# Row-tiled attention scores, stationary exponentials and 0/1 masks in a block-sparse attention with a feed-forward layer behind it

## The chip, the cores and the metric

The kernel runs on one core of one Trainium2 chip. The metric is the device time of one execution in microseconds. Before the change it is 330.93 us (median of 3 runs, 328.9 to 332.64). A lower time is better.

## The reference, cut to what matters

Four batches, eight heads, 768 positions, head size 64. Queries may see keys in blocks of 32: neighbours, the first and last block, and three sampled blocks per query block. The mask is the same for every head and batch. The attention output, with its heads side by side, goes through a feed-forward layer with squared relu.

```python
scores = scale * np.matmul(q, k.transpose(0, 1, 3, 2))
mask = np.abs(blk_i - blk_j) <= 1                       # block = 32
mask = mask | (blk_i == 0) | (blk_j == 0) | (blk_i == n_blocks - 1) | (blk_j == n_blocks - 1)
# ... sampled blocks are set to True per query block
scores = np.where(mask, scores, -1000000000.0)
attn = np.exp(scores - np.max(scores, axis=-1, keepdims=True))
attn = attn / (np.sum(attn, axis=-1, keepdims=True) + 1e-09)
out = np.matmul(attn, v)
# ... x = out with heads side by side: (4 * 768, 512)
h = x @ w_in                                             # 512 -> 2048
g = np.maximum(h, 0.0) ** 2
return g @ w_out                                         # 2048 -> 512
```

## The kernel before

Two heads make one unit, so there are 16 units, four per batch. A unit has three query chunks of 256 and, in each, three key pairs of 2 x 128 keys. One (unit, chunk, pair) is called a slot: 144 in all. Keys lie on the partitions of the scores, so that the exponentials are the moving operand of the second product as they come.

```python
# rows 0..63 of QK hold a head, rows 64..87 hold the mask as 24 more contraction rows
def scores(u, qi, cp):                                   # L319
    # ...
    for c in range(2):
        nc.tensor.matmul(ps[:, c, 0, :], KA[i][0:64 + nb, ksl], QA[i][0:64 + nb, qsl], start=True, stop=True)
        nc.tensor.matmul(ps[:, c, 1, :], KB[i][0:64 + nb, ksl], QB[i][0:64 + nb, qsl], start=True, stop=True)

def exps(u, qi, cp):                                     # ScalarE, 128 x 1024
    nc.scalar.activation(out=pT, in_=stile.pop((u, qi, cp)), func=AF.Exp, scale=scale)

def values(u, qi, cp):                                   # V stationary, half of its columns are ones
    # ...
        nc.tensor.matmul(po[:, 0, :], VA[i][:, n, :], pT[:, c, 0, :], ...)
        nc.tensor.matmul(po[:, 1, :], VB[i][:, n, :], pT[:, c, 1, :], ...)

def inverse(u, qi):                                      # 1/sum on ScalarE: Ln, Ln, Exp(-x)
    nc.scalar.activation(out=ls[0:D, :], in_=po[D:P, 0, :], func=AF.Ln)
    nc.scalar.activation(out=ls[D:P, :], in_=po[0:D, 1, :], func=AF.Ln)
    nc.scalar.activation(out=rs, in_=ls, func=AF.Exp, scale=-1.0)

def normalize(u, qi):                                    # two VectorE multiplies into xT
    V.tensor_mul(out=xT[b][0:D, a, qsl], in0=po[0:D, 0, :], in1=rs[0:D, :])
    V.tensor_mul(out=xT[b][D:P, a, qsl], in0=po[D:P, 1, :], in1=rs[D:P, :])
# feed-forward: hidden on TensorE, relu on VectorE, square on GpSimd, output on TensorE, copy on ScalarE
```

A small list scheduler in the kernel places all these tasks with estimated durations. It fixes the order on each engine when the program is built; every task has one engine.

The softmax here doesn't subtract the row's maximum and nothing guards it: scores larger than these inputs give would overflow.

## Time and profile before

| | before |
|---|---|
| span of the profiled execution | 332.6 us |
| TensorE matmul, busy share | 92% |
| VectorE, ScalarE, GpSimd busy | 157, 210, 129 us |
| matmuls | 2174 |
| DMA transposes | 48 |

The costliest groups of instructions in the page of the kernel before that the change removes or reshapes. A line gives source line, engine, operation, output<-input, shapes, count, then busy us and the mean ns of one, then the engine's idle time just before and what ended it.

```profile
L334 ACT ACTIVATE pT<-ps 128x1024 bf16<-128x1024 f32 x144 | 140.9, 1017 | 41.2 <-PE po L349 32.0
...
L347 PE MATMUL po<-pT,VA 128*128 128x256 bf16 x288 | 71.3, 274 | 7.7 <-DVE xT L368 4.6
L326 PE MATMUL ps<-QK 88*128 88x256 bf16 x288 | 72.6, 277 | 3.0 <-ACT pT L334 1.6
...
L367 DVE TENSOR_TENSOR xT<-po,rs 64x256 bf16<-64x256 f32 x48 | 19.9, 414 | 29.0 <-ACT rs L358 27.3
```

The mean of a matmul here is a latency: 274 ns for 256 columns that follow each other every 109 ns. The share of a matmul in the time is therefore not read from this column, but from the distance of starts. VectorE's wait on `rs` (27.3 us) is the three-step inversion on ScalarE in front of the normalization.

### The profile page before, as it was taken

How to read it: one execution, taken by the hardware profiler on the slowest of the kernel's cores; microseconds unless marked ns; L12 is line 12 of the kernel's file. 1: busy time of each engine (PE TensorE's matmuls, PEld its weight loads, DVE VectorE, ACT ScalarE, POOL GpSimd, SP SyncE). 2: the span in 40 equal slices, each digit the busy share in tenths (PEclk: the TensorE clock that was granted, in tenths of full speed). 3: DMA queues.
4: the chain of work that ended last, by engine and by line, in shares of the span. 5: the costliest groups of instructions: out<-in, count | busy, mean ns of one | idle time of the engine just before them, and what ended most of it. 6: DMA issues, size and time to landing. Idle time of an engine off the chain costs nothing. (4 is left out here: it accounts for less than half of the span.)

```text
span 332.6 us, 5743 instructions
## 1 busy us (share of the span) xinstructions
PE 306.5 (92%) x2174; PEld 209.8 (63%) x2174; DVE 156.6 (47%) x336; ACT 210.2 (63%) x317; POOL 129.3 (39%) x183
## 2 busy tenths in 40 slices
PE   2878899999978978999999999999999999999994
PEld 1555687777855756677776766777776655555541
DVE  7674244885454532366545334344334454444410
ACT  5479897859857778887786978888886301000011
POOL 6157143452422310055444232322223456666610
PEclk9999799999999999999999999999999999999999
DMA  7989995599999997482326200000000000100002
GB/s 228 233 195 206 199 289 211 120 250 229 216 285 239 246 271 225 95 204 42 62 67 73 55 2 32 2 32 3 32 33 1 34 33 32 63 34 32 34 32 96
DMA packets 59561, 39.61 MB, mean 119 GB/s; under 512 B 39790, under 2 KB 56462, under 8 KB 59534
## 3 DMA queue, kind: packets, MB, share of 16 engines
q1 hardware_dynamic: 55038, 34.66, 41.2%
q0 software_dynamic: 4224, 4.19, 7.8%
q10 hardware_dynamic: 272, 0.39, 0.3%
q8 instruction: 17, 0.28, 0.3%
q14 instruction: 10, 0.08, 0.1%
HBM read 27.26 MB, written 6.29 MB: 101 GB/s over the span
## 5 line engine op out<-in xcount | busy, mean ns | idle before, releaser
L395 POOL TENSOR_TENSOR g<-r 128x384 bf16<-128x384 f32 (+1 forms) x144 | 111.0, 776 | 175.7 <-DVE r L389 175.5
L334 ACT ACTIVATE pT<-ps 128x1024 bf16<-128x1024 f32 x144 | 140.9, 1017 | 41.2 <-PE po L349 32.0
L384 PE MATMUL ph<-xT,w_in_sb 128*128 128x384 bf16 (+1 forms) x576 | 120.0, 308 | 2.3 <-DVE r L389 2.1
L389 DVE TENSOR_SCALAR r<-ph 128x384 f32<-128x384 f32 (+1 forms) x144 | 73.1, 512 | 98.3 <-PE ph L384 72.8
L408 PE MATMUL py<-w_out_sb,g 128*128 128x512 bf16 x384 | 110.1, 379 | 0.8 <-ACT ys L413 0.8
L384 PEld LDWEIGHTS <-w_in_sb 128*128 128x128 bf16 x576 | 56.2, 98 | 38.2 <-issue 3.6
L347 PE MATMUL po<-pT,VA 128*128 128x256 bf16 x288 | 71.3, 274 | 7.7 <-DVE xT L368 4.6
L326 PE MATMUL ps<-QK 88*128 88x256 bf16 x288 | 72.6, 277 | 3.0 <-ACT pT L334 1.6
L328 PE MATMUL ps<-QK 88*128 88x256 bf16 x288 | 72.0, 276 | 0.4 <-DVE QK L285 0.2
L349 PE MATMUL po<-pT,VB 128*128 128x256 bf16 x288 | 71.1, 274 | 0.0
L413 ACT COPY ys<-py 128x512 f32<-128x512 f32 x24 | 13.9, 585 | 62.5 <-PE py L408 58.6
L408 PEld LDWEIGHTS <-g 128*128 128x128 bf16 x384 | 37.5, 98 | 22.0 <-issue 1.3
L347 PEld LDWEIGHTS <-VA 128*128 128x128 bf16 x288 | 28.2, 98 | 19.5 <-issue 8.6
L328 PEld LDWEIGHTS <-QK 88*128 88x128 bf16 x288 | 28.6, 99 | 10.4 <-issue 2.3
L326 PEld LDWEIGHTS <-QK 88*128 88x128 bf16 x288 | 28.2, 98 | 9.2 <-issue 1.9
L349 PEld LDWEIGHTS <-VB 128*128 128x128 bf16 x288 | 28.3, 98 | 8.7 <-issue 1.6
L367 DVE TENSOR_TENSOR xT<-po,rs 64x256 bf16<-64x256 f32 x48 | 19.9, 414 | 29.0 <-ACT rs L358 27.3
L356 ACT ACTIVATE ls<-po 64x256 f32<-64x256 f32 x48 | 18.3, 381 | 10.2 <-PE po L349 9.1
L358 ACT ACTIVATE rs<-ls 128x256 f32<-128x256 f32 x48 | 20.0, 416 | 1.5
L368 DVE TENSOR_TENSOR xT<-po,rs 64x256 bf16<-64x256 f32 x48 | 20.5, 427 | 0.6
L357 ACT ACTIVATE ls<-po 64x256 f32<-64x256 f32 x48 | 18.1, 376 | 0.6
L288 DVE CAST CQ<-ks 128x768 bf16<-128x768 f32 x12 | 6.9, 578 | 11.8 <-DMA QK<-CQ 11.7
(49 smaller groups left out, 76.2 us busy)
## 6 DMA issues: line engine op xcount, KB each, us to landing
qs<-in_q_dram SPq DMA_DIRECT2D x16, 384.0 KB, 6.2
vs<-in_v_dram SPq DMA_DIRECT2D x16, 384.0 KB, 8.1
out_dram<-ys SPq DMA_DIRECT2D x24, 256.0 KB, 2.1
ks<-in_k_dram SPq DMA_DIRECT2D x15, 384.0 KB, 8.7
w_in_sb<-in_moe_w_in_dram POOLq DMA_DIRECT2D x4, 512.0 KB, 8.2
w_out_sb<-in_moe_w_out_dram POOLq DMA_DIRECT2D x4, 512.0 KB, 13.4
QK<-CQ SPq DMA_TRANSPOSE x48, 4.0
ks<-in_k_dram ACTq DMA_DIRECT2D x1, 384.0 KB
```

The lines of the kernel that those rows point to most:

```text
L326: nc.tensor.matmul(ps[:, c, 0, :], KA[i][0:64 + nb, ksl], QA[i][0:64 + nb, qsl], start=True, stop=True)
L328: nc.tensor.matmul(ps[:, c, 1, :], KB[i][0:64 + nb, ksl], QB[i][0:64 + nb, qsl], start=True, stop=True)
L334: nc.scalar.activation(out=pT, in_=stile.pop((u, qi, cp)), func=AF.Exp, scale=scale)
L347: nc.tensor.matmul(po[:, 0, :], VA[i][:, n, :], pT[:, c, 0, :], start=first, stop=last, skip_group_check=True)
L349: nc.tensor.matmul(po[:, 1, :], VB[i][:, n, :], pT[:, c, 1, :], start=False, stop=last, skip_group_check=True)
L358: nc.scalar.activation(out=rs, in_=ls, func=AF.Exp, scale=-1.0)
L367: V.tensor_mul(out=xT[b][0:D, a, qsl], in0=po[0:D, 0, :], in1=rs[0:D, :])
L368: V.tensor_mul(out=xT[b][D:P, a, qsl], in0=po[D:P, 1, :], in1=rs[D:P, :])
L384: nc.tensor.matmul(ph, w_in_sb[:, kc, f * P:(f + 1) * P], xT[b][:, kc, c0:c0 + w], start=(kc == 0), stop=(kc == KM - 1))
L389: V.tensor_scalar(out=r, in0=htile.pop((T, f)), scalar1=0.0, scalar2=None, op0=AOP.max)
L395: G.tensor_mul(out=g, in0=r, in1=r)
L408: nc.tensor.matmul(py, gtile[T, f][:, ts * P:(ts + 1) * P], w_out_sb[:, f, :], start=(f == 0), stop=(f == NF - 1))
```

## The change

Its intent: a head has only 64 contraction rows, so half of TensorE's rows can work on the other head at the same time; the second product streams 65 columns (64 of V and one of ones) twice instead of 256 queries once; the mask rows move out of the scores; what VectorE and ScalarE do is spread by the scheduler.

```diff
 def scores(slots, add, e):
-    nc.tensor.matmul(ps[:, c, 0, :], KA[i][0:64 + nb, ksl], QA[i][0:64 + nb, qsl], ...)
-    nc.tensor.matmul(ps[:, c, 1, :], KB[i][0:64 + nb, ksl], QB[i][0:64 + nb, qsl], ...)
+    for h in range(2):                       # rows 0..63 and rows 64..127
+        hs = slice(h * D, (h + 1) * D)
+        nc.tensor.matmul(ps[:, h, c, :], QK[i][hs, 1, ksl], QK[i][hs, 0, qsl], start=c == 0, stop=not add, ...)
+    for h in range(2) if add else ():        # batch 0: additive mask, two more row tiles
+        nc.tensor.matmul(ps[:, h, c, :], oh[hs, ksl], R2[hs, qsl], start=False, stop=True, ...)
+def masks(a, e):                             # batches 1 to 3: 0/1 mask after the exponential
+    V.tensor_tensor(out=pT, in0=pT, in1=m[:, None].broadcast_to([P, 2, 2, QW]), op=AOP.mult)
 def values(a, e):
-    nc.tensor.matmul(po[:, 0, :], VA[i][:, n, :], pT[:, c, 0, :], ...)      # V stationary, 256 columns
+    nc.tensor.matmul(po[:, qc, h, :], pT[:, h, c, qc * P:(qc + 1) * P], VT[i][:, h, n, 0:VW], ...)  # 65 columns
-def inverse(u, qi): ...                      # Ln, Ln, Exp on ScalarE
 def normalize(u, qi, e):
+    V.reciprocal(out=rs, in_=po[:, :, :, D:VW])
+    V.tensor_tensor(out=xq, in0=po[:, :, :, 0:D], in1=rs.broadcast_to([P, 2, 2, D]), op=AOP.mult)
+def x_transp(u, qi, e):                      # queries are on partitions now: transpose back
+    nc.tensor.transpose(pt[:, qc * P:(qc + 1) * P], xq[:, qc].rearrange("p h d -> p (h d)"), identb)
 # ... 12 warm-up matmuls, loads of four units on two queues, half as many DMA transposes
 # scheduler: a task may name several engines, and TensorE pays 0.15 us for a change of tile mode
-    rr = Task("DVE", SQ[w][1], 0, ...relu...)
+    rr = T_({"DVE": 0.48, "ACT": 0.50}, 200, relu, ...)
+    attend(mine[i:i + 2], False)             # scores of two slots in a row from batch 1 on
```

## The prediction

> **What bounds the kernel now.** I read the page first (busy shares, slices), then a table of stretches, the list of waits, the groups by form, and the timeline where matmuls of different shapes meet. A matmul's record includes pipeline latency (about 275 ns for 256 columns), so I take the distance between starts as its cost. The table of stretches; columns: stretch and length, then busy us (instructions) of TensorE matmul, weight load, VectorE, ScalarE, GpSimd, then granted clock, DMA share, GB/s:
>
> ```profile
> 10.00:30.00 20.00, 16.12 (x134) 11.74 (x135) 13.78 (x32) 14.42 (x21) 10.91 (x17) 1.00 0.98 204
> 30.00:60.00 30.00, 28.30 (x230) 22.40 (x228) 12.31 (x31) 25.17 (x37) 10.68 (x18) 0.94 0.94 216
> ...
> 100.00:150.00 50.00, 44.75 (x335) 31.91 (x333) 22.77 (x52) 39.35 (x60) 11.02 (x16) 1.00 0.87 214
> 150.00:200.00 50.00, 50.00 (x373) 36.05 (x372) 24.99 (x51) 39.15 (x59) 21.46 (x25) 1.00 0.27 49
> ```
>
> From 150 us on TensorE never pauses; before that it does. The waits, in us, times, longest:
>
> ```profile
> DVE CQ L288 <- DMA QK<-CQ: 16.8, 11, 4.6
> ...
> PE po L347 <- DVE xT L368: 4.6, 5, 1.7
> ...
> PE pt L278 <- DVE qc L266: 3.0, 2, 1.8
> PE po L347 <- ACT pT L334: 2.9, 4, 1.6
> ```
>
> TensorE waits 21 us in all, 4.8 of them before its first matmul. VectorE, which runs in order, stands 16.8 us behind DMA transposes, and normalization (L367, L368) queues behind that.
>
> Matmul starts follow each other by 108 to 110 ns for 256 columns, 162 for 384, 216 for 512, 55 for a 128-column transpose (0.50 us for six): columns at full clock plus 2 to 3 ns. So TensorE's stream is scores 576 x 0.109 = 63, second product the same 63, hidden 384 x 0.162 + 192 x 0.109 = 83, output 384 x 0.216 = 83, transposes 3: **295 of 332.6 us**. TensorE bounds it. By landmarks: attention of batch 0 (36 slots of three query chunks by three key pairs) ends near 66 us; that of batches 1 to 3 near 263, for 180 us of stream; then 62 us of pure feed-forward to 328, and 5 us of copy and store.
>
> **What the Trainium skill says.** "TensorEngine Tiling (Array Packing)", Key Properties, says that tiles run independently and that changing the tiling mode drains the array. "TensorE: Matmul & The Clock Gate", Part 3, has row groups start about 4 ns apart and finish together, so two 64-row matmuls should cost one. No run here shows that yet. The drain may be visible once, where the 24-row transposes (L254) stand between 88-row matmuls:
>
> ```profile
> 27.27 0.27 PE L328 MATMUL ps<-QK 88*128 88x256 bf16 x1
> ...
> 27.47 0.21 PEld L254 LDWEIGHTS <-QK 24*128 24x128 bf16 x6 [0.21 <-issue]
> 27.48 0.31 PE L254 MATMUL pc<-identb,QK 24*128 24x24 bf16 x6
> ...
> 27.71 0.10 PEld L326 LDWEIGHTS <-QK 88*128 88x128 bf16 x1
> ```
>
> L254 follows 0.205 us after a matmul whose columns take 0.108: 0.097 lost. The next weight load comes 0.096 us after the last L254 start (27.616), where it normally comes 2 ns after. I estimate **0.095 us per switch**.
>
> The same group settles weight loads. "TensorE: Matmul & The Clock Gate", LDWEIGHTS, gives P / 1.2 ns, 107 for 128 columns; but these six pairs, each with its own 128-column load, follow each other by 25 ns (0.31 less 0.17 for one record, over five, is 28). The measurement decides: a load hides behind a 65-column matmul, which should cost 65 / 2.4 + 2.5 = **30 ns** (estimate).
>
> "SBUF — State Buffer", Who interferes with whom: a VectorE instruction with two SBUF inputs locks out a GpSimd instruction that reads SBUF and the reverse, for the whole instruction, as do VectorE's two-port copies. The trace agrees for copies: one cast takes 0.56 us free, and 0.97 when GpSimd started first:
>
> ```profile
> 58.46 0.98 POOL L395 TENSOR_TENSOR g<-r 128x256 bf16<-128x256 f32 x1 [0.49 <-DVE r L389]
> ...
> 58.89 0.97 DVE L288 CAST CQ<-qs 128x768 bf16<-128x768 f32 x1
> ...
> 115.24 0.56 DVE L288 CAST CQ<-ks 128x768 bf16<-128x768 f32 x1 [1.74 <-DMA QK<-CQ]
> ```
>
> "VectorE: DVE Perf Modes", perf-mode tier table, gives bf16 tensor_tensor in SBUF two elements per cycle; with the page's fixed 151 cycles a mask multiply of 1024 elements is (512 + 151) / 0.96 = **0.69 us** (estimate; the trace before has no such instruction).
>
> **The change, part by part.** Counts are from the built order of both kernels.
>
> Scores: 576 matmuls become 288 concurrent pairs: 63 to 31 us. Batch 0 keeps the additive mask, 72 more pairs, +8.
> Second product: 576 x 0.109 becomes 1152 x 0.030: 63 to 35.
> New on TensorE: 96 transposes of x, 5; mask tiles, 2; 184 mode switches x 0.095, 17.5. Hidden and output stay. New stream: 295 - 24 - 28 + 7 + 17.5 = **268 us**; so switches eat over half of what row tiling gives.
> ScalarE: loses three inversion steps per (unit, query chunk), 18.3 + 18.1 + 20.0 = 56 us; gains some 32 relus, and some copies of x. Exponentials stay (about 0.905 us from start to start though 1.017 recorded).
> VectorE: loses 40 us of normalization (L367, L368) and part of the relus; gains 108 masks, 75 us, and 48 reciprocal-and-multiply pairs at about 0.17 + 0.41.
> DMA: 48 transposes become 24, the mask rows vanish, loads start earlier and on two queues; only DMA and waits become shorter by it.
>
> By stage of the new order (stream totals 40.5 + 16.2 + 134.6 + 76.4):
> A. To the end of batch 0's 36 slots: stream 40.5 us, of which 64 switches 6. ScalarE needs 36 x 0.905 = 33 plus evacuations, now without the inversions (12 x 1.17 = 14 us of its queue here). The first slots still wait for loads; the last unit's keys come at about 21 us at today's 230 GB/s, so slot 12 ends near 26 and the other 24 take about 1.05 us each: **51 us** instead of 66.
> B. Feed-forward of batch 0 until unit 4 begins: **16 us**, TensorE alone.
> C. Slots 37 to 144: stream 134.6. VectorE in the same stretch: masks 108 x 0.69 = 74.5, normalization 35 x 0.58 = 20, 35 relus 18, copies and casts 15: **128 us** with no waiting. GpSimd holds the shared port here for about 63 squares (19 x 0.61 + 44 x 0.83 = 48) and 12 casts. So it is busy some 40% of the stretch; a mask that meets it waits half an instruction, 0.4 us: 108 x 0.4 x 0.4 = 17. VectorE becomes 145, and in-order gaps make that about **150 us**, over TensorE's 135. Today this part takes 197.
> D. Feed-forward after the last values: **76 us** (62 now: attention has run ahead), with no waits today in that kind of stretch, and 5 of tail.
> Sum: 51 + 16 + 150 + 76 + 5 = 298; I add 3 for waits that the schedule brings at its x transposes: **301 us**. So of 30 us saved, 27 are stream and the rest is waiting, with the VectorE ceiling in C taking back what TensorE would gain further.
>
> **Rivals.**
> 1. *VectorE does not bind.* If port conflicts are rare, stage C is TensorE's 135 plus a few waits: 288. For it: VectorE's waits on DMA, 16.8 us, shrink. Against: 128 us of its own work in 135 leaves no slack.
> 2. *Masks at one element per cycle*, because of the broadcast operand: (1024 + 151) / 0.96 = 1.22 us, +57 on VectorE: about 355, slower. The innermost step is 1 in all operands, so I give it 3%.
> 3. *Row tiles do not overlap.* Pairs cost two matmuls: 360 x 0.109 = 39 more, 23 of them in C, where VectorE hides 15, and perhaps 8 in A: about 317.
> 4. *Short matmuls bound by weight loads.* At 50 ns instead of 30, +23 us of stream, 17 in C, of which VectorE hides most: about 308. At the recorded 98 ns each, +78: slower; but the 25 and 55 ns spacings exclude that.
> 5. *Transposes of x stall TensorE.* They stand in its order behind VectorE's normalization, 48 times with a single accumulator; 0.4 us each would be 19. ScalarE's part of today's chain (about 1.2 us) is gone, so I count 3.
>
> **Range and chances.** Rivals 1 and 3 to 5 span 288 to 318, and they can partly add. I say 288 to 318. Faster by over 2% (below 324) 0.94; within 2% 0.04; slower 0.02, which needs rival 2 or two others together.
>
> **What would show it.** Right: pairs of score matmuls with starts a few ns apart and 110 ns to the next pair; about 30 ns between 65-column matmuls; about 0.1 us lost at each switch; masks near 0.69 us alone and about 1.1 beside GpSimd; VectorE over 90% busy between roughly 67 and 217 us, with TensorE waiting on masks there; TensorE without waits after. Wrong: masks above 1 us throughout; 200 ns per pair; TensorE full in C, or waits on loads or on x's transposes as the largest item.

## The result, and the profile after

The changed kernel takes **309.09 us** (median, 308.72 to 310.17, 4 runs) against 331.78 us for the kernel before in the same rounds (330.93 without its run of 334.18 us, which is over 1.5% above the fastest, counts as slow and is left out of the ratio). The ratio is 0.9348, with a 95% interval of 0.9299 to 0.9397. A ratio here is the mean time of one kernel's fast runs over that of the other's of the same rounds, so it is not quite the ratio of the medians quoted. The result passed the comparison with the reference, which is all that "correct" means below. The profiled execution is listed with 309.11 us; its span from first to last instruction is 307.4 us.

The table of stretches after the change, with the same cuts and columns as the one of before in the prediction:

```profile
10.00:30.00 20.00, 17.63 (x272) 12.07 (x271) 12.12 (x27) 15.94 (x19) 7.07 (x10) 1.00 1.05 217
30.00:60.00 30.00, 29.22 (x447) 20.50 (x447) 15.04 (x42) 22.44 (x26) 8.28 (x13) 1.00 0.94 244
...
100.00:150.00 50.00, 44.28 (x541) 25.17 (x542) 42.47 (x81) 37.93 (x47) 25.64 (x27) 1.00 0.41 100
150.00:200.00 50.00, 47.72 (x586) 27.41 (x583) 41.07 (x81) 40.04 (x51) 22.55 (x22) 1.00 0.07 22
```

VectorE (third number) went from 22.8 to 42.5 us in the stretch from 100 to 150, and the DMA share fell from 0.87 to 0.41. TensorE is now not full between 150 and 200 us either, where it was full before.

The list of waits after the change (us, times, longest):

```profile
PEld L366 <- DVE pT L350: 15.4, 33, 0.9
...
PE po L366 <- DVE pT L350: 6.3, 16, 0.6
...
PE po L382 <- DVE xq L375: 3.6, 7, 0.7
```

The exponentials are stationary now, so it is the weight load (PEld) of the second product that stands before a mask that is not done. None of the waits in these lines reaches 1 us, while TensorE's three in the prediction's list had longest ones of 1.6 to 1.8 us. (The longest wait of TensorE after the change, 1.8 us, is for a mask tile in the first 10 us.) VectorE's wait for DMA transposes (16.8 us before) is gone.

The timeline where shapes meet (start, length, engine, line, count):

```profile
130.77 0.65 PE L403 MATMUL ph<-xT,w_in_sb 128*128 128x384 bf16 x3
131.25 0.79 PE L366 MATMUL po<-VT,pT 128*128 128x65 bf16 x16
131.97 0.61 PE L333 MATMUL ps<-QK 64*128 64x256 bf16 x8
```

Sixteen 65-column matmuls, whose records last 0.19 us, span 0.79 us: starts 29 ns apart at the median, some at 35 to 39, and once 154 where the second slot waits for VectorE. Eight score matmuls span 0.61 us, of which 0.27 is the last one's latency. That leaves 0.34 for the starts: in the trace they are 131.975, 131.978, 132.094, 132.097, 132.203, 132.207, 132.312 and 132.316, so pairs 3 to 4 ns apart with 109 ns from pair to pair once the first has run. The last of the sixteen starts at 131.852 and its 65 columns take 0.030 us, so 0.093 us pass before the first score matmul: this is what a change of tile mode (from matmuls on 128 rows to matmuls on 64, or back) costs.

From the page: the masks and relus on VectorE, the second product on TensorE, and the two instructions on VectorE that replaced the inversion and the old normalization:

```profile
L350 DVE TENSOR_TENSOR pT<-pT,MK 128x1024 bf16<-128x1024 bf16 x108 | 87.2, 822 | 6.5 <-ACT pT L343 6.4
L412 DVE TENSOR_SCALAR r<-ph 128x384 f32<-128x384 f32 (+1 forms) x112 | 57.1, 513 | 42.1 <-POOL g L421 24.0
...
L366 PE MATMUL po<-VT,pT 128*128 128x65 bf16 x1152 | 54.0, 194 | 8.2 <-DVE pT L350 6.3
...
L373 DVE RECIPROCAL rs<-po 128x4 f32<-128x4 f32 x48 | 8.6, 179 | 29.8 <-PE po L366 29.7
L375 DVE TENSOR_TENSOR xq<-po,rs 128x256 bf16<-128x256 f32 x48 | 20.4, 424 | 1.7
```

And the shared port, answering to the casts of before: a mask alone, and one beside GpSimd (timeline).

```profile
85.82 0.68 DVE L350 TENSOR_TENSOR pT<-pT,MK 128x1024 bf16<-128x1024 bf16 x1
...
90.98 1.63 POOL L421 TENSOR_TENSOR g<-r 128x256 bf16<-128x256 f32 x2 [0.96 <-DVE r L412]
...
91.01 1.13 DVE L350 TENSOR_TENSOR pT<-pT,MK 128x1024 bf16<-128x1024 bf16 x1
```

The 34 masks that no GpSimd record overlaps last 0.683 us on average; the 74 that one overlaps last 0.886 us.

**Where the time went.** I add up TensorE's stream as columns / 2.4 + 2.5 ns per matmul (which gives the spacings of 55, 109, 162 and 216 ns that the prediction read for 128 to 512 columns), a side-by-side pair counted once, and 0.093 us per change of tile mode. Stages are the ones of the prediction, cut at the last or first matmul of the second product.

| stage | before us (stream) | predicted | after us (stream + mode changes) |
|---|---|---|---|
| A, to the last values of batch 0 | 74.7 (52.8) | 51 | 54.5 (36.1 + 6.0) |
| B, until unit 4's first values | 3.5 (2.9) | 16 | 17.6 (16.0 + 0.2) |
| C, until the last values | 186.3 (176.3) | 150 | 154.8 (122.4 + 11.0) |
| D, feed-forward alone | 63.5 (62.1) | 76 | 76.2 (76.2) |
| tail | 4.6 | 5 | 4.2 |
| sum | 332.6 (294.1) | 298, +3 | 307.3 (267.9) |

The stream fell by 26 us. What is not stream was 38.5 us and is 39.4 us, but it moved: in stage A it fell from 21.9 to 12.4 us, and in stage C it rose from 10.0 to 21.4. In stage A a part of this is TensorE's clock, which the prediction did not count: in the trace before, 256-column matmuls start 0.21 us apart up to 14.4 us and again from 34.9 to 38.3 us, where the granted clock is 0.5; after the change the clock is full from 4.3 us on. The matmuls that ran at half clock before would take 4.8 us at full clock, so I estimate that up to 5 us of stage A's gain is this; no run separates it from the earlier loads. Of the 21.4 us in stage C that are neither stream nor mode change, 17.8 are pauses of over 15 ns: 11.9 before a matmul of the second product, 5.3 before a transpose of x, 0.7 elsewhere. Both wait on VectorE.

### The profile page after: what moved, and what is told of

Read it like the earlier page. It is cut to its first block, busy times and chain, and to the rows that moved or that the text cites. A ratio compares the mean times of both kernels' runs of the same rounds, so it can differ in the third digit from the quotient of the medians.

```text
span 307.4 us, 7318 instructions
## 1 busy us (share of the span) xinstructions
PE 284.8 (93%) x3002; PEld 166.2 (54%) x3002; DVE 203.1 (66%) x411; ACT 172.0 (56%) x217; POOL 152.6 (50%) x187
## 4 chain that ended last, share of the span: by engine, by line
PE 59%; DVE 19%; ACT 10%; issue 5%; DMA 3%; POOL 2%; SPq 0%; ACTq 0%; DVEq 0%; POOLq 0%
PE ph L403 21%; PE py L433 20%; DVE pT L350 10%; PE po L366 7%; ACT pT L343 7%; PE ps L333 7%; DVE r L412 3%; DVE qc L158 2%; DVE xq L375 2%; POOL g L421 2%; DMA qs<-in_q_dram 2%; PE po L382 2%; PE ps L337 2%; DMA vs<-in_v_dram 1%; ACT MK L268 1%
## 5 line engine op out<-in xcount | busy, mean ns | idle before, releaser
L421 POOL TENSOR_TENSOR g<-r 128x384 bf16<-128x384 f32 (+1 forms) x144 | 125.0, 877 | 119.4 <-DVE r L412 96.0
L350 DVE TENSOR_TENSOR pT<-pT,MK 128x1024 bf16<-128x1024 bf16 x108 | 87.2, 822 | 6.5 <-ACT pT L343 6.4
L412 DVE TENSOR_SCALAR r<-ph 128x384 f32<-128x384 f32 (+1 forms) x112 | 57.1, 513 | 42.1 <-POOL g L421 24.0
L366 PE MATMUL po<-VT,pT 128*128 128x65 bf16 x1152 | 54.0, 194 | 8.2 <-DVE pT L350 6.3
L366 PEld LDWEIGHTS <-pT 128*128 128x128 bf16 x1152 | 44.1, 98 | 30.5 <-DVE pT L350 15.4
L333 PE MATMUL ps<-QK 64*128 64x256 bf16 x576 | 52.1, 272 | 1.8 <-ACT pT L343 0.8
L333 PEld LDWEIGHTS <-QK 64*128 64x128 bf16 x576 | 24.2, 94 | 18.4 <-issue 11.6
L375 DVE TENSOR_TENSOR xq<-po,rs 128x256 bf16<-128x256 f32 x48 | 20.4, 424 | 1.7
L410 ACT ACTIVATE r<-ph 128x384 f32<-128x384 f32 (+1 forms) x32 | 14.5, 454 | 8.0 <-PE ph L403 7.5
L337 PE MATMUL ps<-R,oh 64*128 64x256 bf16 x144 | 17.7, 269 | 0.0
```

The lines of the kernel that those rows point to most:

```text
L333: nc.tensor.matmul(ps[:, h, c, :], QK[i][hs, 1, ksl], QK[i][hs, 0, qsl], start=c == 0, stop=not add, skip_group_check=True)
L337: nc.tensor.matmul(ps[:, h, c, :], oh[hs, ksl], R2[hs, qsl], start=False, stop=True, skip_group_check=True)
L350: V.tensor_tensor(out=pT, in0=pT, in1=m[:, None].broadcast_to([P, 2, 2, QW]), op=AOP.mult)
L366: nc.tensor.matmul(po[:, qc, h, :], pT[:, h, c, qc * P:(qc + 1) * P], VT[i][:, h, n, 0:VW], start=(n == 0 and qc == 0 and h == 0), stop=n ...
L375: V.tensor_tensor(out=xq, in0=po[:, :, :, 0:D], in1=rs.broadcast_to([P, 2, 2, D]), op=AOP.mult)
L412: V.tensor_scalar(out=r, in0=src, scalar1=0.0, scalar2=None, op0=AOP.max)
```

## The experiments

Theory V says that TensorE's pauses in stage C come from VectorE and its masks, lengthened by the port that it shares with GpSimd. Rival L says that they come from the order of instructions, the two score buffers and ScalarE. Other runs take parts of the change apart. No run undoes the new form of the second product or the move of the inversion; their part in the gain rests on the stream alone and is not shown by an experiment. Every run's ratio is to the kernel before in its own rounds; the changed kernel has 0.9348, and 0.9323 when run again.

### Without the masks

```diff
 def masks(a, e):
+    return
     u, qi, cp = a
```

> The 108 mask multiplies on VectorE are left out; every other instruction keeps its place (wrong result on purpose, attention of batches 1 to 3 is not masked). Theory V (VectorE, with its 87 us of masks, holds back TensorE in the stretch from the first mask to the last values, which lasts 154.8 us with 17.8 us of TensorE stalls): the stretch falls to 137 to 141, the median from 309 to 292 to 297. Rival L (the stalls come from the order of instructions, the two score buffers and ScalarE's exponentials): at most 5 us, 304 or more.

Measured: 293.01 us (291.8 to 293.25), ratio 0.8843; wrong result. Stage C in the table of stretches:

```profile
73.20:211.10 137.90, 137.49 (x1766) 85.14 (x1764) 52.67 (x142) 119.17 (x154) 60.84 (x79) 1.00 0.40 99
```

The stretch is 137.9 us, within the expected 137 to 141, and TensorE is full in it, with ScalarE as busy as before (119 us). The order was kept, so the order, the score buffers and ScalarE do not cause the pauses without the masks: theory V holds, and rival L falls as the sole cause. The run does not show that the pauses are the masks' in any order; the run with measured costs below bears on that.

### Squares that read no SBUF

```diff
-            (G if e == "POOL" else V).tensor_mul(out=g, in0=r, in1=r)
+            G.memset(g, 1.0)
```

> GpSimd's squares become memsets, which read no SBUF (wrong result on purpose); order unchanged. If the masks are slow because a VectorE instruction with two SBUF inputs and a GpSimd instruction that reads SBUF lock each other out, the mask's mean falls from 822 ns to about 690 to 720, VectorE has about 11 us less, and the median falls by 4 to 9 us, to 300 to 305. If the masks take 0.82 us for another reason, mean and time stay within 2 us.

Measured: 300.02 us by median of four, the three fast runs 299.37 to 300.31; ratio 0.9056. The profiled run: TensorE at half clock for 6.8 us in stage A, so I take no time of a stage from it, only the group of masks on VectorE:

```profile
L350 DVE TENSOR_TENSOR pT<-pT,MK 128x1024 bf16<-128x1024 bf16 x108 | 75.8, 715 | 8.3 <-ACT pT L343 8.0
```

The mean went from 822 to 715 ns. GpSimd still reads SBUF in its casts. In this trace the 23 masks that only a memset overlaps last 685 ns on average, as those alone do; in the changed kernel the 57 that only a square overlaps last 848. So the slow masks are those that meet a reading GpSimd instruction. The time gained, 9 us, is at the upper end of what was expected; the memsets are also shorter than the squares (418 against 927 ns at 384 columns), which frees relu buffers sooner, so not all 9 us need be the port's.

### The additive mask for all batches

```diff
-                attend(mine[i:i + 2], False)
+                attend(mine[i:i + 2], True)
 # likewise the last slot of a unit
```

> Undoes one part: no 0/1 masks on VectorE, batches 1 to 3 add the mask on TensorE with two more row-tiled pairs per slot, as batch 0 does, and the scheduler orders anew. TensorE gains 108 x 2 x 0.109 = 23.5 us of stream, VectorE loses 87 us. Theory V: the stalls of 17.8 us vanish but the stream is longer: 309 + 23.5 - 15 = 317, between 312 and 322. Rival L: stalls stay, about 330.

Measured: 316.24 us, ratio 0.9549, correct. The moved masks cost TensorE 23.5 us of stream, yet the whole is only 7 us slower than the changed kernel. In stage C TensorE's pauses of over 15 ns come to 0.4 us, against 17.8 with masks on VectorE. So the 0/1 masks are worth 7 us in this kernel, not the 23.5 that they take from TensorE.

### The additive mask for every third group

```diff
-                attend(mine[i:i + 2], False)
+                attend(mine[i:i + 2], i // 2 % 3 == 1)
```

> Every third group of two slots in batches 1 to 3 adds its mask on TensorE, the others multiply on VectorE. TensorE +7 us of stream (about 32 slots x 0.218), VectorE -26 us. Theory V: stalls fall from 17.8 to 5 or so, about 304, between 300 and 308, faster than the changed kernel. Rival L: 314 to 317.

Measured: 304.39 us (303.46 to 306.39), ratio 0.9214, correct. A unit has four groups of two slots and a single one, so the edit moves one group in each unit, 24 of the 108 slots (22%, not the third or about 32 that was expected): 84 masks remain on VectorE. Pauses of over 15 ns in stage C are 7.3 us instead of 17.8. The wait for masks, in the list of waits:

```profile
PE po L366 <- DVE pT L350: 2.2, 6, 0.6
```

It was 6.3 us. This version beats the changed kernel: the interval of its ratio, 0.9155 to 0.9273, lies below that of 0.9299 to 0.9397.

### Score groups of one slot

```diff
-            for i in range(0, len(mine) - 1, 2):
-                attend(mine[i:i + 2], False)
-            # ... the last slot of a unit
+            for a in mine:
+                attend([a], False)
```

> Scores of batches 1 to 3 are issued one slot at a time instead of two: nearly twice as many changes of tile mode there. Each change costs TensorE 93 ns in the trace. If that cost is real on the path, up to 50 more excursions x 2 x 0.093 = 9 us of stream; where VectorE holds TensorE back part of it hides: 311 to 318. If the 93 ns are an artefact of the records, or the single slot lets ScalarE flow better, the time stays at 306 to 310.

Measured: 322.55 us, ratio 0.9735. This is slower than expected, and not by the mode changes: the scheduler put neighbouring groups together by itself, so the built program has 218 changes instead of 186 (both with two at the very start), 32 x 0.093 = 3 us. The rest shows in the waits:

```profile
PE po L382 <- DVE xq L375: 15.6, 25, 1.5
```

TensorE stands 15.6 us before transposes of x whose normalization is not done, against 3.6. With this order there is less feed-forward inside stage C (its stream there is 89.6 us) and more after it (109.5). So what this run shows is how much the placement of other work matters; the cost of a mode change on the path it does not isolate.

### All of one head, then all of the other

```diff
+        if not add:
+            # ...
+            for h in range(2):
+                for a, ps in zip(slots, pss):
+                    for c in range(2):
+                        nc.tensor.matmul(ps[:, h, c, :], ...)   # rows h * 64 .. h * 64 + 63
```

> The same score matmuls of batches 1 to 3, but all of head 0 of a group and then all of head 1, so that only the last of one overlaps the first of the other: 7 units of 0.109 us instead of 4 per group of two slots, 54 groups, at most +18 us of stream. If row tiles run side by side only when neighbours in the order use different rows: the spacing within a head is 109 ns, and the time rises by 8 to 18 us (317 to 327), less what VectorE's stalls hide. If the array reorders or the gain was not from overlap: 307 to 311.

Measured: 311.62 us, ratio 0.9415. The eight matmuls still span what they did before (timeline):

```profile
130.58 0.62 PE L333 MATMUL ps<-QK 64*128 64x256 bf16 x8
```

In the built program four matmuls of rows 0 to 63 come first, then four of rows 64 to 127. In the trace the starts are 130.581, 130.595, 130.701, 130.715, 130.811, 130.824, 130.919 and 130.932: pairs 13 to 14 ns apart. The semaphores tell which is which. In the program the increment for the first slot is on the sixth matmul and the third waits for the second score buffer; in the trace the fourth record carries the increment and the fifth the wait. So the array started the fifth instruction before the third: two row groups run apart from each other in the queue. My first reading of what this edit would do was wrong, and it cannot say what the overlap is worth. The next run does.

### Both heads on the same rows

```diff
+                    hs = hs if add else slice(0, D)
                     nc.tensor.matmul(ps[:, h, c, :], QK[i][hs, 1, ksl], QK[i][hs, 0, qsl], ...)
```

> Both heads' scores of batches 1 to 3 are computed from rows 0 to 63 (head 1 gets head 0's scores: wrong result on purpose), so that no two of them can run side by side; counts, sizes and tile mode stay. It follows heads_in_turn, where the trace still showed pairs 14 ns apart although the program put four matmuls of one head first. If side-by-side running is what row tiling gives: starts 109 ns apart, +23.5 us of TensorE stream, of which at most 15 hide in the stalls behind VectorE: 318 to 330. If the array would have paired them anyway or the gain is elsewhere: within 3 us of 309.

Measured: 320.59 us, ratio 0.9661, against 309.69 and 0.9323 for the changed kernel in the same rounds. Head 1 gets head 0's scores, so the result is wrong; the comparison with the reference still passed, so it does not notice such an error. The timeline:

```profile
131.64 1.04 PE L334 MATMUL ps<-QK 64*128 64x256 bf16 x8
```

The eight matmuls now span 1.04 us, 109 ns from start to start. Stage C's stream is 145.7 instead of 122.4 us and its length 165.7 instead of 154.8: of 23.3 us of stream, 11 show in the time. The other 12 fill pauses behind VectorE. Running side by side is real, and half of its gain in these batches is lost to waiting.

### The scheduler with measured costs

```diff
-SWITCH = 0.15
+SWITCH = 0.093
-            ex = T_(("DVE", 0.6), s - 1, masks, ...)
+            ex = T_(("DVE", 0.82), s - 1, masks, ...)
-            va = T_(("PE", 0.40), s + 2.2, values, ...)
+            va = T_(("PE", 0.24), s + 2.2, values, ...)
```

> Only three numbers of the scheduler change, to what the trace shows: 0.24 us for a slot of the second product (was 0.40), 0.093 for a change of mode (0.15), 0.82 for a mask (0.60). Instructions are the same, their order moves. If a wrong model makes TensorE meet its waits: 2 to 8 us faster, 301 to 307. If VectorE's throughput bounds the stretch whatever the order: within 2 us of 309.

Measured: 307.33 us (306.97 to 307.95), ratio 0.9289. That is 1.8 us less than the changed kernel by the medians, but in other rounds, and the intervals of the ratios overlap. The time alone does not decide between the two answers. The granted clock has a part in it: its mean was 0.977 to 0.983 in all four runs, against 0.992 to 1.000 for the changed kernel. In the profiled run it was 0.5 from 119.9 to 130.2 us, in stage C; the matmuls started there would take 3.8 us at full clock, so I estimate that about 4 us were lost. Outside that stretch the pauses of over 15 ns in stage C are 11.2 us, against 17.8. So the order does have a part in the pauses, and the clock hid most of this gain. Why the clock fell is not shown.

### One warm-up matmul

```diff
-    N_WARM = 12
+    N_WARM = 1
```

> One warm-up matmul instead of twelve. If the twelve bring the clock up before the first real matmuls: a stretch at half clock of about 3.4 us in the first 15 us and 0.5 to 2.5 us more in time (309.5 to 311.5). If the start waits for loads anyway: within 0.7 us.

Measured: 310.06 us, ratio 0.9365 (0.9322 to 0.9407), against 0.9348 (0.9299 to 0.9397). In its trace the clock is full only from 13.2 us on, against 4.3 with twelve, and six transposes at about 7 us take 0.82 us instead of 0.51. So the twelve do bring the clock up earlier; in time it is about 1 us at most, which the intervals do not separate from nothing.

### One engine per task again

```diff
-    RELU = {256: {"DVE": 0.35, "ACT": 0.42}, 384: {"DVE": 0.48, "ACT": 0.50}}
+    RELU = {256: {"DVE": 0.35}, 384: {"DVE": 0.48}}
 # likewise: copies of x and casts of q and k on VectorE alone, output copies on ScalarE alone
```

> Undoes the choice of engines: all relus, copies of x and casts of q and k on VectorE, output copies on ScalarE. VectorE gets some 28 relus (14 us), 12 copies (3) and 10 casts (6) more in the stretch with masks, where it is busy 130 of 155 us. Theory V: 12 to 22 us slower, 321 to 331. Rival L (order and ScalarE bound the stretch): ScalarE loses 17 us, so 304 to 312.

Measured: 312.64 us (312.61 to 316.39), ratio 0.9444: 3 us slower than the changed kernel in the same rounds, where 12 to 22 were expected. VectorE's busy time in stage C rose from 130.4 to 144.1 us, while the stage lasted 152.9 us in the profiled execution. The profiled execution was the slowest of the four: its granted clock was 0.5 from 10.0 to 16.8 us, in stage A, and 0.988 in the mean, against 1.000 in the other three. The scheduler ordered anew and moved feed-forward behind stage C (stage D lasts 81.1 us instead of 76.2), so the stage's length alone does not tell; TensorE's pauses of over 15 ns in it rose from 17.8 to 20.8 us. The time is just above rival L's 304 to 312. So VectorE still had slack, which took nearly all of the added work. This corrects theory V: VectorE is not full in the changed kernel. TensorE waits for it because a mask stands in line, not because VectorE has no time left.

### Every third group, with measured costs; and the changed kernel again

The edits of two earlier runs together, five rounds, beside the changed kernel unaltered on the same chip.

> The two edits that helped, together: every third group adds its mask on TensorE, and the scheduler has the three measured costs. Gains add if one takes work from VectorE and the other only places what is left: 300 to 304. If they are the same stalls: 303 to 306.

> The changed kernel itself, on the same chip and in the same rounds as third_true_costs, for a comparison below 1%: 308 to 311.

Measured: 304.89 us (302.6 to 306.48), ratio 0.9179 (0.9128 to 0.9230), correct; the changed kernel 309.69 us (308.83 to 309.84), ratio 0.9323 (0.9275 to 0.9371). The intervals do not overlap: it is about 1.5% faster than the changed kernel and 8% faster than the kernel before. Against every third group alone (0.9214) there is no difference to be seen. This agrees with the second expectation, that the two edits remove the same pauses. A small further gain is not excluded: the mean granted clock was 0.983 to 0.989 in five of the six runs, and the sixth, at 1.000, took 302.6 us.

## Why the prediction was right, and where it was off

It said 301 us with a range of 288 to 318, and faster; the median is 309.09. TensorE's stream and its waits for masks were as stated; the limit that the prediction set for stage C was not. Term by term:

**TensorE's stream.** Predicted 268 us, and 267.9 by the table. Both are counts of the built program times a cost for each kind, so what the trace tests is the costs. They held: 65-column matmuls at 29 ns by the median (31 in the mean where they wait for nothing), pairs side by side, and a mode change at 93 ns by the median of 184 of them, where 95 was estimated from one group of 24-row matmuls in the trace before. The built program confirms that that group ran in another tile size. Mode changes cost 17 us.

**Stage A.** Predicted 51 us, traced 54.5. Slot 12 was put near 26 us and came at 29.0. TensorE's pauses there are around the mask tiles and the first evacuations (2.3 us before the first mask tiles alone), a part that the prediction did not time. The landmark of 66 us that it gave for this stage before was the end of the exponentials; the last values of batch 0 came at 74.7 us, behind feed-forward work.

**Stage B.** 17.6 us against 16; 1.4 us of pauses.

**Stage C.** Predicted 150 us with VectorE as its limit, traced 154.8. The step that failed is "VectorE becomes 145, and in-order gaps make that about 150": VectorE is busy for 130.4 us there, 84% and not over 90. The mis-sized term is the sum: added up record by record, VectorE's work there is 143.9 us, as predicted, but the end of one record overlaps the start of the next, so that 130.4 us are occupied. The port's part, predicted as 108 x 0.4 x 0.4 = 17 us, came to 74 x 0.203 = 15, from two errors that cancel: 69% of the masks meet GpSimd and not 40%, and each loses 0.2 us and not 0.4. What it underrated is the price of standing in line: TensorE pauses for 17.8 us although VectorE has 24 us free. The runs without masks, with squares that read no SBUF and with 24 of the masks elsewhere (-16, -9 and -5 us) show that VectorE's masks make these pauses, the run with measured costs that the order has a part in them, and the run with one engine per task (+14 us of VectorE work for +3 us of time) that a full VectorE does not. So it is partly luck that 150 came near 154.8: VectorE's time was put too high by 15 us, and the 21.4 us that are neither stream nor mode change there came from its queue instead.

**Stage D and tail.** 76.2 and 4.2 us against 76 and 5.

**The allowance.** 3 us were added for waits at the transposes of x; they are 5.3 us, already within stage C above. Finally the listed time is 1.7 us longer than the span that the sum describes. From 301 to 309: +3.5 in A, +1.6 in B, +4.8 in C, -0.6 in D and tail, -3 for the allowance, +1.7: 8.0.

**The rivals.** VectorE that does not bind (288) had VectorE's busy time nearly right (128 us of its own work) and the time wrong. Masks at one element per cycle did not come: 0.683 us alone, where 0.69 was estimated with the fixed part of the Trainium skill's "VectorE: DVE Perf Modes". Row tiles overlap, and short matmuls are not bound by weight loads. Transposes of x stall TensorE, but by 5 us and not 19.

## What to carry to other kernels

When a change takes work from the bounding engine and gives part of it to another, price the other engine's queue as well as its sum: here 84% busy was enough to stall TensorE for 18 us, because each result stood in line behind others and behind a shared port. How the work is ordered changes that price, so a new order is worth a run. Count the mode changes that a tiled matmul brings (here 17 us, over half of what side-by-side scores saved); what placing them in groups gains, no run here isolates. And where an operation can run on either of two engines, a mixture can beat both pure choices: 24 of 108 masks on TensorE gave 304 us, none gave 309, all gave 316.

## What the Trainium skill lacked or had wrong

- "TensorE: Matmul & The Clock Gate", the part on loading the stationary operand, gives P / 1.2 ns, 107 for 128 columns. The record of one load is near that (98 ns here), but the 1152 65-column matmuls, each with its own load of 128 columns, followed each other every 29 ns by the median. So the formula is not the distance between loads.
- The same page says that matmuls stay in program order. With all matmuls of one row group ahead of the other's, the fifth started 14 ns after the first and 0.2 us before the third (the run with one head after the other).
- "TensorEngine Tiling (Array Packing)" says that a change of mode drains the array, and gives no cost. Here it is 93 ns by the median, in either direction.
- "SBUF — State Buffer" has the lock between a VectorE instruction with two SBUF inputs and a GpSimd instruction that reads SBUF; it gives no cost for this pair. For a 128 x 1024 bf16 multiply it was 0.683 us alone and 0.886 us on average when GpSimd overlapped it.
